# Score products of a Mamba-2 chunk: eight of 128 columns, row tiles innermost, in place of four of 256

## The chip, the cores and the metric

The kernel runs on one core of a Trainium2 chip. The metric is device time in microseconds (us) of one launch, as the median over runs. Engines are named as the profile names them: PE is TensorE's matmul side, PEld its weight loads, DVE is VectorE, ACT is ScalarE, POOL is GpSimd, SP issues most of the DMAs.

## The reference

Two blocks follow each other, all in fp32. The first is a chunked state-space scan over 4 sequences of 768 tokens, 8 heads, head size 32 and state size 16. The second sends its 3072 x 256 result through four experts.

```python
# scan, per chunk of tokens (i, j inside the chunk)
L  = exp(cum[i] - cum[j]) * (i >= j)
CB = einsum('bhin,bhjn->bhij', Cc, Bc)          # the scores
y  = (CB * L) @ xc  +  (Cc @ state) * exp(cum)  # within the chunk + from before it
state = decay_full * state + sum_j decay_from_j * outer(Bc, xc)
# experts, x = y as (3072, 256)
p = domain_probs / sum(domain_probs)
for e in range(4):
    out += p[:, e] * (relu(x @ w1[e]) @ w2[e])  # w1: 256 x 1024, w2: 1024 x 256
```

## The kernel before

The scan is done in 24 chunks of 128 tokens (`c`), four chunks to a block of 512 tokens (`k`, six blocks). The experts are done per block in eight steps (`n`, 48 in all): each step takes one expert and one part of its hidden units. From step 2 on, the two layers are done with seven products each in place of eight (`fmul`, `smul`, with sums of weights made by POOL and sums of activations by DVE); the first two steps are plain. Products of the first layer go to the PSUM banks `X` and `Y`, those of the second are summed in four banks `acc0` to `acc3`. Two more banks (`att`) serve the scan.

The order of the work on every engine is the order of the source (a manual schedule): nothing is moved by a planner. The main loop at line 734 runs over `n`; chunks of the next block enter at steps 0, 2, 4 and 6 (`c_in`) and leave a step later (`c_out`).

A chunk goes through these functions:

- `masks` (L357, ACT) makes `ctm`: C transposed (8 heads x 16 states = 128 rows, 128 tokens), twice. In copy `t` only the rows of heads with parity `t` are kept, so that a group of 32 rows (`q`, two heads) yields one head's scores for each `t`.
- `scores` (L366, PE) makes the scores. A product of group `q` has the 32 x 128 block of B as its stationary operand and the 32 rows of `ctm` as the moving one. It runs in a row tile of the array (`tile_position=(32 * q, 0)`), and the four groups write four different PSUM banks, `g`. From chunk 4 on the banks are `att`, `att`, `X`, `Y`.
- `masked` (L376, DVE) multiplies each `g` by the decays `LT` into `MT`; from chunk 4 on in the order of q = 2, 3, 0, 1, so that `X` and `Y` are read first.
- `outputs` (L389 and L395, PE; L401 and L404, ACT) makes the chunk's outputs. L395 works in column tiles: eight products, `t` outside and `q` inside, of 144 columns (128 in the last block).

In the main loop `scores` and `masked` stand behind `smul(n - 1, 2)` and ahead of `diff(n, "T3", ...)`, `smul(n - 1, 4)`, and the next step's `opened` (`fmul` 1 into `X`, `fmul` 2 into `Y`). Every fp32 product that is no transpose shows in the profile as two weight loads and two matmuls, called two passes here: the 96 score products are 192 records.

The gate of the first expert is spread by four products of 128 columns with stationary operands of 128 columns in the full height of the array (L278, `spread_gate`, 96 rows).

Of the kernel before, what the change touches and what calls it, by code (L numbers as in the profile page):

```python
# [8 lines left out]
FP32 = mybir.dt.float32  # L9
# [3 lines left out]
P = 128  # L13
NQ, NT = 4, 2
# [3 lines left out]
def kernel(  # L18
# [37 lines left out]
    nc = tc.nc  # L56
# [10 lines left out]
    OB, OBT, OCT = DM, DM + HN, DM + 2 * HN  # L67
# [119 lines left out]
    for t, queue in enumerate((nc.sync, nc.scalar)):  # L187
        queue.dma_start(
            out=a_q.rearrange("(q r) c t s -> q r c (t s)", q=NQ)[:, t],
            in_=a.rearrange("(i k) (q t) s -> k q i (t s)", k=NBLK, t=NT)[0][:, 0:SPREAD])  # L190
    nc.scalar.dma_start(
        out=a_sb, in_=a.rearrange("c h s -> (c h) s").rearrange("(p r) s -> p r s", r=2))
# [166 lines left out]
    def scores(c, homes):  # L359

        s = st[c]
        s["g"] = []
        for q, (pool, tag) in enumerate(homes):
            k = slice(32 * q, 32 * q + 32)
            g = pool.tile([P, NT, P], FP32, tag=tag, name="g")
            nc.tensor.matmul(  # L366
                out=g.rearrange("p t s -> p (t s)"), lhsT=s["xb"][k, OBT:OBT + P],
                rhs=s["ctm"][k].rearrange("p t s -> p (t s)"),
                start=True, stop=True, tile_position=(32 * q, 0))
            s["g"].append(g)  # L370

    def masked(c, qs):
        s = st[c]
# [270 lines left out]
    homes = ((ps_s, "acc0"), (ps_s, "acc1"), (ps_att, "att"), (ps_att, "att"))  # L644
# [12 lines left out]
    turn(1, 1)  # L657
    masks(0)
    scores(0, homes)
    decays(0)  # L660
    spread(1)
# [4 lines left out]
    decays(1)  # L666
    turn_gates()
    scores(1, banks)
    masks(2)
    spread(2, (0,))  # L670
# [10 lines left out]

    plain_first(0, 1, (0,))
    scores(2, homes)
    plain_first(0, 1, (1,))
    decays(2)
# [48 lines left out]
    for n in range(PLAIN, NS):  # L734
        k, r = divmod(n, SPB)
# [131 lines left out]
```

## Time and profile before

| | |
|---|---|
| median of 6 runs | 657.29 us (656.55 to 659.99) |
| the profiled execution | 656.26 us, its span 654.5 us |
| granted TensorE clock, mean | 0.998 |
| PE busy | 645.7 us (99% of the span), 3367 records |
| PEld busy | 541.9 us (83%), 3367 records |
| DVE, ACT, POOL busy | 483.9, 115.8, 109.9 us |
| score matmuls (L366) | 192 records, median 478 ns, first at 6.8 us, last at 531.4 us |

The span is the time from the first to the last instruction; the launch's own time is 1.76 us longer. A matmul's record is longer than its turn in the array, since matmuls are pipelined: four matmuls in a row of 256 columns show as 379 ns each, but start 216 ns apart. So starts are read here, not durations. A record of a first matmul behind a change of tiling begins together with its weight load.

### The profile page before, as it was taken

The numbers are of one execution on the slowest core, as the hardware profiler recorded it, in microseconds if no ns is written. First come the engines' busy times: TensorE is split into PE (matmuls) and PEld (weight loads), VectorE is DVE, ScalarE is ACT, GpSimd is POOL, SyncE is SP. The second block draws the span as 40 slices with busy tenths as digits, with TensorE's granted clock in tenths as the row PEclk, the third lists the DMA queues.
The fourth block names the chain that finished last, engine by engine and source line by source line (L and its number), as shares of the span: only waits on it lengthen the run. The fifth ranks groups of instructions, "written<-read, shape, count | busy, mean of one in ns | idle before, by whom it ended". The sixth has DMA issues, their size and how long they took to land.

```text
span 654.5 us, 8922 instructions
## 1 busy us (share of the span) xinstructions
PE 645.7 (99%) x3367; PEld 541.9 (83%) x3367; DVE 483.9 (74%) x814; ACT 115.8 (18%) x247; POOL 109.9 (17%) x157
## 2 busy tenths in 40 slices
PE   8999989999999999999999999999999999999997
PEld 5788868888888888888888888888888888888886
DVE  8679879779686687786867867768777676756555
ACT  2111111221112122111221121112211212111110
POOL 4798383020000002000002000000100000100000
PEclk9999999999999999999999999999999999999999
DMA  7979999542767451666843478536066553156000
GB/s 233 330 274 362 316 383 346 201 162 84 237 197 289 176 192 55 213 235 232 254 162 122 131 247 279 195 130 242 13 239 205 225 187 129 59 162 223 0 1 32
DMA packets 68138, 126.83 MB, mean 194 GB/s; under 512 B 26600, under 2 KB 50048, under 8 KB 68096
## 3 DMA queue, kind: packets, MB, share of 16 engines
q1 hardware_dynamic: 65152, 111.10, 49.6%
q0 software_dynamic: 2304, 14.68, 5.6%
q8 instruction: 26, 0.43, 0.3%
q10 hardware_dynamic: 640, 0.49, 0.2%
q14 instruction: 16, 0.13, 0.1%
HBM read 108.18 MB, written 18.07 MB: 193 GB/s over the span
## 4 chain that ended last, share of the span: by engine, by line
PE 95%; DMA 2%; POOL 1%; DVE 0%; issue 0%; SPq 0%; ACT 0%; POOLq 0%
PE acc L534 41%; PE X L449 23%; PE Y L449 18%; PE g L366 3%; PE y L395 2%; PE acc L515 2%; DMA wt<-in_w_dram 1%; PE y L389 1%; PE X L498 1%; PE Y L498 1%; PE a L309 1%; DMA xb<-in_xbc_dram 1%; POOL wt L161 0%; POOL wt L162 0%; POOL wt L160 0%
## 5 line engine op out<-in xcount | busy, mean ns | idle before, releaser
L461 DVE TENSOR_TENSOR z<-Y,snap 128x512 f32<-128x512 f32 x138 | 94.7, 686 | 127.5 <-ACT snap L456 83.1
L534 PE MATMUL acc<-hT,wt 128*128 128x256 f32 x736 | 183.1, 382 | 0.0
L456 ACT COPY snap<-X 128x512 f32<-128x512 f32 x138 | 80.9, 586 | 466.3 <-PE X L449 466.3
L534 PEld LDWEIGHTS acc<-hT,wt 128*128 128x128 f32 x736 | 138.3, 190 | 24.0 <-issue 6.0
L449 PE MATMUL X<-yS,wt 128*128 128x256 f32 x552 | 141.7, 379 | 0.0
L534 PE MATMUL acc<-h,wt 128*128 128x256 f32 x552 | 141.5, 379 | 0.0
L534 PEld LDWEIGHTS acc<-h,wt 128*128 128x128 f32 x552 | 104.9, 190 | 14.3
L449 PEld LDWEIGHTS X<-yS,wt 128*128 128x128 f32 x552 | 104.9, 190 | 14.3
L471 DVE SCALAR_TENSOR_TENSOR h<-z,gate 128x512 f32<-128x512 f32 x138 | 97.5, 707 | 3.5 <-PE acc L515 0.4
L449 PE MATMUL Y<-yT,wt 128*128 128x256 f32 x368 | 94.5, 379 | 0.0
L449 PEld LDWEIGHTS Y<-yT,wt 128*128 128x128 f32 x368 | 68.6, 189 | 10.8 <-DVE z L461 0.2
L478 DVE TENSOR_TENSOR hT<-h,hT 128x512 f32<-128x512 f32 x92 | 66.5, 722 | 1.6
L478 DVE TENSOR_TENSOR hT<-h,h 128x512 f32<-128x512 f32 x92 | 63.9, 719 | 0.8
L343 DVE TENSOR_TENSOR_SCAN LT<-ab,ident 128x512 f32<-128x512 f32 x42 | 52.4, 1248 | 0.1
L449 PE MATMUL Y<-yS,wt 128*128 128x256 f32 x184 | 49.3, 390 | 0.0
L348 POOL TENSOR_TENSOR MT<-xb,LT 128x128 f32<-128x128 f32 x20 | 8.6, 429 | 240.5 <-PE Y L449 125.4
L449 PE MATMUL X<-yT,wt 128*128 128x256 f32 x184 | 47.2, 379 | 0.0
L376 DVE TENSOR_TENSOR MT<-g,LT 128x256 f32<-128x256 f32 x96 | 34.0, 417 | 16.5 <-PE g L366 16.4
L329 POOL TENSOR_TENSOR cts<-ctm,dec 128x256 f32<-128x256 f32 x20 | 19.7, 983 | 155.5 <-ACT snap L456 155.5
L449 PEld LDWEIGHTS Y<-yS,wt 128*128 128x128 f32 x184 | 33.3, 189 | 8.1 <-issue 4.2
L471 DVE SCALAR_TENSOR_TENSOR h<-X,gate 128x512 f32<-128x512 f32 x50 | 34.3, 686 | 7.7 <-PE X L449 4.1
L449 PEld LDWEIGHTS X<-yT,wt 128*128 128x128 f32 x184 | 35.0, 190 | 4.8
(94 smaller groups left out, 339.4 us busy)
## 6 DMA issues: line engine op xcount, KB each, us to landing
wt<-w_d SPq DMA_DIRECT2D x80, 896.0 KB, 8.9
w_d<-wt POOLq DMA_DIRECT2D x16, 896.0 KB, 6.4
ab<-acut_d SPq DMA_DIRECT2D x21, 512.0 KB, 6.1
wt<-in_w_dram SPq DMA_DIRECT2D x32, 256.0 KB, 6.2
xb<-in_xbc_dram SPq DMA_DIRECT2D x24, 320.0 KB, 5.0
gate<-p_d SPq DMA_DIRECT2D x23, 256.0 KB, 8.3
out_dram<-ot SPq DMA_DIRECT2D x160, 16.0 KB, 4.8
ah<-ac_d SPq DMA_DIRECT2D x20, 64.0 KB
```

Of the source, the lines that this page charges most:

```text
L329: nc.gpsimd.tensor_mul(cts, s["ctm"], dec.unsqueeze(1).to_broadcast([HN, NT, P]))
L343: nc.vector.tensor_tensor_scan(out=LT[:, i * w:i * w + w], data0=s["a"][i], data1=ident.rearrange("p h s -> p (h s)")[:, :w], initial=0.0, ...
L366: nc.tensor.matmul(out=g.rearrange("p t s -> p (t s)"), lhsT=s["xb"][k, OBT:OBT + P], rhs=s["ctm"][k].rearrange("p t s -> p (t s)"), start ...
L376: nc.vector.tensor_mul(s["MT"][:, h, 0:P], s["g"][q], s["LT"][:, h])
L395: nc.tensor.matmul(out=y[32 * q:32 * q + 32, t, 0:w], lhsT=xb[:, h * D:h * D + D], rhs=MT[:, NT * q + t, 0:w], start=(first and t == 0), s ...
L449: nc.tensor.matmul(out=f[bank][:, j], lhsT=wt1[n][:, w, j * P:j * P + P], rhs=rhs, start=(i in (1, 2, 5) and j == 0), stop=(j == JJ - 1), ...
L456: nc.scalar.copy(out=s, in_=first[n]["X"])
L461: nc.vector.tensor_add(z, first[n]["Y"], first[n][i])
L471: nc.vector.scalar_tensor_tensor(out=h, in0=first[n][src], scalar=0.0, in1=g.unsqueeze(1).to_broadcast([P, JJ, HB]), op0=ALU.max, op1=ALU. ...
L478: nc.vector.tensor_sub(h[o], h[x], h[y])
L498: nc.tensor.matmul(out=f[bank][:, j], lhsT=wt1[n][:, w, j * P:j * P + P], rhs=yT[k][:, i, cols], start=(i == 0 and j == 0), stop=(i == 1), ...
L534: nc.tensor.matmul(out=acc[k, u][:, half], lhsT=w2_op(n, w)[:, j], rhs=rhs[:, j], start=(begins and j == 0), stop=(n % SPB == SPB - 1 and ...
```

## The change

The four `g` tiles are allocated first. Then the products are issued with `t` outside and `q` inside, each over one `t` half of the moving operand and of the tile: eight products of 128 columns in place of four of 256. The stationary operand of a group is the same for both `t`, and is loaded for each product. Only the product with `t == 0` has the start flag; both have the stop flag.

```diff
         s = st[c]
         s["g"] = []
-        for q, (pool, tag) in enumerate(homes):
-            k = slice(32 * q, 32 * q + 32)
-            g = pool.tile([P, NT, P], FP32, tag=tag, name="g")
-            nc.tensor.matmul(
-                out=g.rearrange("p t s -> p (t s)"), lhsT=s["xb"][k, OBT:OBT + P],
-                rhs=s["ctm"][k].rearrange("p t s -> p (t s)"),
-                start=True, stop=True, tile_position=(32 * q, 0))
-            s["g"].append(g)
+        for pool, tag in homes:
+            s["g"].append(pool.tile([P, NT, P], FP32, tag=tag, name="g"))
+        for t in range(NT):
+            for q, g in enumerate(s["g"]):
+                k = slice(32 * q, 32 * q + 32)
+                nc.tensor.matmul(
+                    out=g[:, t], lhsT=s["xb"][k, OBT:OBT + P], rhs=s["ctm"][k, t],
+                    start=(t == 0), stop=True, tile_position=(32 * q, 0), skip_group_check=True)
```

## The prediction

> **What bounds the kernel now.** I read the page's busy shares first, then its chain, then the timeline around one chunk's scores.
>
> ```profile
> PE 645.7 (99%) x3367; PEld 541.9 (83%) x3367; DVE 483.9 (74%) x814; ACT 115.8 (18%) x247; POOL 109.9 (17%) x157
> ...
> PE 95%; DMA 2%; POOL 1%; DVE 0%; issue 0%; SPq 0%; ACT 0%; POOLq 0%
> PE acc L534 41%; PE X L449 23%; PE Y L449 18%; PE g L366 3%; PE y L395 2%; PE acc L515 2%; DMA wt<-in_w_dram 1%; PE y L389 1%; PE X L498 1%; PE Y L498 1%; PE a L309 1%; DMA xb<-in_xbc_dram 1%; POOL wt L161 0%; POOL wt L162 0%; POOL wt L160 0%
> ```
>
> TensorE is the bound nearly everywhere: a nanosecond added to the scores (3% of the chain) moves the end by a nanosecond, unless something else waits there. 24 chunks pass, so 0.3% of the median, 1.97 us, is 82 ns per chunk. That 0.3% is also about what a measurement of this kernel can tell from no change.
>
> Next, PE's timeline around the scores of a chunk of the main loop, then the matmuls and loads of L366 that lie in six short stretches (number in brackets: records that overlap the stretch):
>
> ```profile
> 136.82 0.38 PE L534 MATMUL acc<-h,wt 128*128 128x256 f32 x1
> 137.13 0.71 PE L366 MATMUL g<-ctm,xb 32*128 32x256 f32 x8
> 137.77 0.70 PE L534 MATMUL acc<-hT,wt 128*128 128x256 f32 x2
> ```
>
> ```profile
> core 0: us, PE busy (x) PEld busy (x), PEclk, DMA share, GB/s
> 137.12:137.16 0.04, 0.03 (x4) 0.03 (x4) 1.00 0.51 205
> 137.16:137.23 0.07, 0.07 (x4) 0.07 (x4) 1.00 0.56 227
> 137.23:137.26 0.03, 0.03 (x4) 0.03 (x8) 1.00 1.19 495
> 137.26:137.44 0.18, 0.18 (x4) 0.18 (x8) 1.00 0.52 208
> 137.44:137.48 0.04, 0.04 (x8) 0.00 (x0) 1.00 0.00 0
> ```
>
> The eight passes of the four products run as two rounds of four. All four row tiles start within 20 ns (137.12 to 137.16); the loads of the second pass start 107 ns later (137.23 to 137.26); the second four matmuls start at 137.45, which is 0.32 us after the first records: a load of 107 ns and a stream of 256 columns of 213 ns. So the tiles already run side by side, and the second round's loads already hide under the first round's streams. The burst, start to start, takes 644 ns (137.13 to 137.77): 107 load, 2 x 213.5 stream, 20 stagger of the four tiles, 90 until the next tiling's first load. Record by record, 21 of the 24 chunks show these numbers within 1 ns.
>
> **What a round of 128 columns costs.** What remains is whether a round of half the columns takes half the time: its stream is 107 ns, as long as its load. Two places show neighbouring cases: four products of 128 columns with full loads of 128 columns (L278), and eight products in column tiles, `t` outside and `q` inside as in the change (L395).
>
> ```profile
> 15.31 0.97 PEld L278 LDWEIGHTS gp<-p_sb,ident 96*128 96x128 f32 x8 [0.23 <-issue]
> ```
>
> ```profile
> 143.58 0.70 PE L395 MATMUL y<-MT,xb 128*32 128x144 f32 x16
> 144.21 1.13 PE L449 MATMUL Y<-yS,wt 128*128 128x256 f32 x4
> ```
>
> L278: eight loads in 0.97 us, the last one 190 ns long, so seven steps in 0.78 us: 111.4 ns a step. Load and 128-column stream overlap there, and the pair costs 4.5 ns more than the load alone. L395: sixteen passes in four rounds. The last record is 286 ns, so the last start is 0.41 us after the first: a load of 27 ns (32 columns), three steps of 122 ns, a stagger of 20 ns. 144 columns stream in 120 ns at the rate of 256 in 213.5, so the rounds cost 2 to 3 ns beyond their streams. That row shows that eight products in tiles with this loop order fall into rounds of four, and that twice as many instructions keep the 20 ns stagger.
>
> **The sum, part by part.** Removed: two streams of 213.5 ns per chunk, 427 ns. Added: four rounds in their place, with eight more loads and eight more matmuls (192 each over the kernel). A round costs 107 ns if only the stream counts, and 213.5 ns if four row tiles that load while four others stream take as long as the trace can hide: the second round's loads had 213 ns to finish in, and the trace does not show when within it they were done. I take the L278 step, 111.4 ns: it has the same load, the same stream and the same overlap, only the tiling differs; the loads of the first round, four at once, took 107 ns as well, so that tiles loading side by side do not slow each other. The burst then is 107 load + 3 x 111.4 + 107 last stream + 20 stagger + 90 until the next load = 658 ns, against 644: +14.5 ns. The ends are +1 ns (3 x 107) and +320 ns (3 x 213.5 and the last stream 107).
>
> Over the kernel: 23 chunks x 14.5 ns = 0.33 us. Chunk 0 runs at half the clock (its second round starts 588 ns after the first in place of 320), so its share doubles to about 0.03 us or a little more. In chunks 3 and 4 a bank comes free late, and the last tiles start 0.65 us and 0.40 us after the first; the late tiles then need four rounds in place of two, +14.5 ns again, while the early tiles' second halves ride along. In all +0.4 us; by the ends 0.0 and +7.7 us.
>
> The allocation of the four tiles ahead of the products costs nothing: each bank's wait stays with its group's first product. What is new is that a wait of group 2 or 3 now has second halves queued behind it that did not exist before; in the main loop no such wait shows (all four start within 20 ns), and where one shows (chunks 3, 4) it is priced above.
>
> Who waits for the scores: DVE, idle 0.92 us ahead of `masked` in the main loop.
>
> ```profile
> 137.92 1.42 DVE L376 TENSOR_TENSOR MT<-g,LT 128x256 f32<-128x256 f32 x4 [0.92 <-PE g L366]
> 138.53 0.84 PEld L449 LDWEIGHTS X<-yT,wt 128*128 128x128 f32 x4
> 138.74 1.03 PE L449 MATMUL X<-yT,wt 128*128 128x256 f32 x4
> ```
>
> The first mask reads `X` until about 138.34, and PE writes `X` again from 138.74: 0.4 us of room. Since DVE and PE shift together with the burst's end, +14.5 ns is not felt; the next `Y` (139.60, its mask done at 138.67) has more room still. No DMA, ACT or POOL instruction moves.
>
> So the profiled execution would go from 654.5 to 654.9 us of span and from 656.26 to 656.7 of its own time. The median of the runs is 1.03 us above that execution: 657.29 + 0.4 = 657.7.
>
> [...]
>
> **The rivals.**
>
> *Loads only partly hidden (slower).* Four tiles loading while four stream has 107 ns to hide in instead of 213, and no row shows it at that pace. If a load under streams takes longer than alone, each of three steps grows. It decides from a step of 134 ns (111.4 + (82 - 14.5)/3). The price reaches from there to +320 ns per chunk, 7.7 us; the middle, a step of 160 ns, is +3.9 us, 661.2. Against it: L278's full-height step of 111.4, and loads under streams that show 184 ns as records against 181 without. For it: nothing but the missing row.
>
> *The second halves do not join the burst (slower).* If TensorE doesn't let a tile's second product follow while other tiles still work, one more drain and load fall between `t = 0` and `t = 1`: 90 + 107 = 0.2 us per chunk, 4.7 us, 662.0. L395 speaks against it: there the second `t` follows without a gap. It is column tiles, though, with loads of 27 ns.
>
> *Less around the burst (faster).* The last full matmul's stream ends at 137.03 (136.82 + 0.216) and the next begins at 137.88 (137.77 + a load of 0.107): 0.85 us, of which 0.43 are streams, so 0.42 are not. Around L395 the same reading (143.06 + 2 x 0.216 = 143.49 to 144.32) gives 0.83 - 4 x 0.122 = 0.34. If smaller products had the smaller share, 77 ns x 24 = 1.8 us would go, 655.5, at the edge of the bound. Most of that difference is the first load (107 against 27 ns), which stays.
>
> That the change doesn't do what it says (loads left out because the stationary operand repeats) is nearly excluded: between two loads of one operand three others come, and it would give at most the forecast's 0.4 us back.
>
> **How the numbers follow.** Forecast case 0.62, its own range 656.3 to 659.0 (both ends of the small terms and the runs' scatter). Partly hidden loads 0.20, spread from 659.3 to 665.0. Second halves apart 0.10, near 662.0. Faster 0.08. So faster by over 0.3% is 0.08, within 0.3% 0.62, slower 0.30. The range 656.0 to 663.0 leaves out most of the faster case and the dearer part of the partly hidden loads, together 0.15 to 0.2. The prediction is the likeliest case's 657.7.
>
> **What would show it.** In the changed kernel L366 has 384 matmul records and 384 loads. Right: sixteen passes in four rounds, starts 111 ns apart, the burst from first L366 record to the next L534 record 0.66 us, DVE's wait ahead of `masked` within 0.03 us of 0.92. Partly hidden: rounds 134 ns or more apart. Apart: a gap of 0.2 us inside the burst between the eighth and the ninth matmul. Wrong altogether: a burst of 0.66 us and yet a time outside 655.3 to 659.3, or a new wait of PE for `X` or `Y`.

## Result and the profile after

The changed kernel takes 657.96 us (median of 36 runs, 656.3 to 660.19), against 657.23 us of the kernel before (78 runs). The ratio is 1.0015 with a 95% interval of 1.0010 to 1.0021: 0.15% slower, +1.0 us (0.7 to 1.4), inside the 0.3% that the prediction counts as no change. The profiled execution took 657.68 us, its span 655.9 us.

The page of the changed kernel, busy shares and chain:

```profile
PE 645.6 (98%) x3559; PEld 547.2 (83%) x3559; DVE 482.0 (73%) x814; ACT 115.8 (18%) x247; POOL 110.9 (17%) x157
...
PE 94%; DMA 2%; DVE 2%; SPq 1%; issue 1%; POOL 0%; ACT 0%; POOLq 0%
```

192 matmuls and 192 loads more, and TensorE is still the bound. The same burst as in the prediction (chunk 8, in the main loop), on PE's timeline, and its score records in short stretches (in brackets the records that overlap each):

```profile
137.81 0.59 PE L534 MATMUL acc<-h,wt 128*128 128x256 f32 x2
138.33 0.73 PE L368 MATMUL g<-ctm,xb 32*128 32x128 f32 x16
138.99 0.48 PE L534 MATMUL acc<-hT,wt 128*128 128x256 f32 x1
```

```profile
138.32:138.36 0.04, 0.03 (x4) 0.03 (x4) 1.00 0.42 179
138.36:138.43 0.07, 0.07 (x4) 0.07 (x4) 1.00 0.34 125
138.43:138.47 0.04, 0.04 (x4) 0.04 (x8) 1.00 0.08 26
138.54:138.58 0.04, 0.04 (x8) 0.04 (x8) 1.00 0.08 26
138.65:138.69 0.04, 0.04 (x12) 0.04 (x8) 1.00 0.04 13
138.76:138.80 0.04, 0.04 (x12) 0.04 (x4) 1.00 0.08 26
```

Four matmul records overlap at first, eight in the second round and twelve from the third on (a record, median 270 ns, is longer than its turn of 107 to 112 ns a round), and a new four begins every 0.11 us; the rounds' loads lie under the streams of the round before. Record by record, the first load takes 107 ns, the loads of the rounds begin 109 and then 112 ns apart, and the next L534 begins 657 ns after the first score record, against 644 before: +13 ns. DVE waits 0.90 us for the scores, as before (0.92):

```profile
139.11 1.42 DVE L376 TENSOR_TENSOR MT<-g,LT 128x256 f32<-128x256 f32 x4 [0.90 <-PE g L368]
```

**Nothing else grew from chunk 7 on.** The bursts of chunk 7 and chunk 23 (the last) on PE's timeline, first of the kernel before, then of the changed one:

```profile
110.86 0.71 PE L366 MATMUL g<-ctm,xb 32*128 32x256 f32 x8
...
531.04 0.71 PE L366 MATMUL g<-ctm,xb 32*128 32x256 f32 x8
```

```profile
112.05 0.73 PE L368 MATMUL g<-ctm,xb 32*128 32x128 f32 x16
...
532.43 0.73 PE L368 MATMUL g<-ctm,xb 32*128 32x128 f32 x16
```

From the one to the other are 420.18 us before and 420.38 after: 0.20 us for 16 bursts, 13 ns each (12.5 at the rows' rounding). From chunk 7 to the end of the span it is 654.47 - 110.86 = 543.61 against 655.86 - 112.05 = 543.81. The profiles of the runs below agree: 543.60 to 543.62 us wherever chunks 7 to 23 have four products, 543.81 to 543.82 wherever they have eight in this order. What the two profiled executions differ by otherwise, 1.2 of 1.4 us, lies ahead of 112 us.

**Where it lies.** At 88 us PE waits for chunk 6's `cts` (C times the decays, the moving operand of the product at L389), which POOL makes late, behind sums of weights. PE's timeline of the kernel before has there 2.55 us:

```profile
90.41 0.70 PE L389 MATMUL y<-cts,M 128*128 128x256 f32 x2 [2.55 <-POOL cts L329]
```

and the changed kernel's has 2.55 us too:

```profile
89.96 0.70 PE L389 MATMUL y<-cts,M 128*128 128x256 f32 x2 [2.55 <-POOL cts L329]
90.59 0.99 PE L395 MATMUL y<-MT,xb 128*32 128x144 f32 x16
91.51 2.08 PE L449 MATMUL Y<-yS,wt 128*128 128x256 f32 x4
```

POOL is late because a transfer of weights (`wt<-in_w_dram`) lands near 80 us. The first sum of weights that waits for it, on POOL's timeline, before and then after:

```profile
80.26 0.72 POOL L160 TENSOR_TENSOR wt<-wt 128x256 f32<-128x256 f32 x1 [9.49 <-DMA wt<-in_w_dram]
```

```profile
79.74 0.72 POOL L160 TENSOR_TENSOR wt<-wt 128x256 f32<-128x256 f32 x1 [9.13 <-DMA wt<-in_w_dram]
```

From there POOL needs 10.1 and 10.2 us to the end of `cts`. In the kernel before, the chain that ends this wait goes back over POOL's sums, that transfer (70.99 to 80.09 us), its issue and DVE to PE's own work up to 68 us.

The four L449 matmuls behind the wait take 2.08 us in the changed kernel; with nothing in their way four take 1.13. The clock was halved: busy times and granted clock of two stretches of the changed kernel (PE, PEld, DVE, ACT, POOL; then the clock):

```profile
87.45:90.85 3.40, 0.89 (x10) 0.56 (x14) 3.37 (x3) 0.00 (x0) 3.00 (x6) 1.00 1.01 422
90.86:94.26 3.40, 3.40 (x23) 2.42 (x14) 0.98 (x3) 0.46 (x2) 3.00 (x5) 0.50 1.02 426
```

The halved stretch lasts 3.41 us and pushes all later products back by 1.6 us (from the wait's end to chunk 7 it is 22.09 us, against 20.45).

The start differs too, and also by the clock. Eight matmuls of L309, behind chunk 0's scores, on PE's timeline before and after:

```profile
7.95 3.30 PE L309 MATMUL a<-a_q,qmask 128*128 128x256 f32 x8
```

```profile
6.89 1.99 PE L309 MATMUL a<-a_q,qmask 128*128 128x256 f32 x8
```

The trace's record of the full clock begins at 10.64 us before and at 5.52 us after, which is ahead of the first changed instruction (6.12 us). Chunk 1 begins at 11.29 and 10.54 us.

So the profiled pair differs by bursts (+0.2 from chunk 7 on), by the halved stretch (+1.6), and by a start that is 0.45 us ahead when the wait ends. Only the first belongs to the change for certain. The runs that follow ask how much of the measured +1.0 us it is.

### The profile page after: what moved, and what is told of

Read it like the earlier page. It is cut to its first block, busy times and chain, and to the rows that moved or that the text cites. A ratio compares the mean times of both kernels' runs of the same rounds, so it can differ in the third digit from the quotient of the medians.

```text
span 655.9 us, 9306 instructions
## 1 busy us (share of the span) xinstructions
PE 645.6 (98%) x3559; PEld 547.2 (83%) x3559; DVE 482.0 (73%) x814; ACT 115.8 (18%) x247; POOL 110.9 (17%) x157
## 4 chain that ended last, share of the span: by engine, by line
PE 94%; DMA 2%; DVE 2%; SPq 1%; issue 1%; POOL 0%; ACT 0%; POOLq 0%
PE acc L534 41%; PE X L449 23%; PE Y L449 18%; PE y L395 2%; PE g L368 2%; PE acc L515 2%; DMA wt<-in_w_dram 2%; PE y L389 1%; PE X L498 1%; PE Y L498 1%; DMA wt<-w_d 1%; DVE LT L343 1%; DVE h L471 0%; PE t L651 0%; SPq L133 0%
## 5 line engine op out<-in xcount | busy, mean ns | idle before, releaser
L534 PE MATMUL acc<-hT,wt 128*128 128x256 f32 x736 | 183.1, 382 | 0.0
L534 PEld LDWEIGHTS acc<-hT,wt 128*128 128x128 f32 x736 | 138.3, 190 | 20.2
L449 PE MATMUL X<-yS,wt 128*128 128x256 f32 x552 | 142.1, 380 | 0.0
L534 PE MATMUL acc<-h,wt 128*128 128x256 f32 x552 | 141.5, 379 | 0.0
L449 PEld LDWEIGHTS X<-yS,wt 128*128 128x128 f32 x552 | 105.3, 191 | 14.5
L534 PEld LDWEIGHTS acc<-h,wt 128*128 128x128 f32 x552 | 104.9, 190 | 14.3
L449 PE MATMUL Y<-yT,wt 128*128 128x256 f32 x368 | 94.5, 379 | 0.0
L449 PEld LDWEIGHTS Y<-yT,wt 128*128 128x128 f32 x368 | 68.7, 190 | 10.7 <-DVE z L461 0.2
L478 DVE TENSOR_TENSOR hT<-h,hT 128x512 f32<-128x512 f32 x92 | 65.0, 706 | 1.6
L449 PE MATMUL Y<-yS,wt 128*128 128x256 f32 x184 | 50.2, 396 | 0.0
L449 PE MATMUL X<-yT,wt 128*128 128x256 f32 x184 | 47.2, 379 | 0.0
L449 PEld LDWEIGHTS Y<-yS,wt 128*128 128x128 f32 x184 | 33.8, 192 | 8.5 <-issue 3.9
L449 PEld LDWEIGHTS X<-yT,wt 128*128 128x128 f32 x184 | 35.0, 190 | 4.8
```

The source lines that it names most:

```text
L449: nc.tensor.matmul(out=f[bank][:, j], lhsT=wt1[n][:, w, j * P:j * P + P], rhs=rhs, start=(i in (1, 2, 5) and j == 0), stop=(j == JJ - 1), ...
L478: nc.vector.tensor_sub(h[o], h[x], h[y])
L534: nc.tensor.matmul(out=acc[k, u][:, half], lhsT=w2_op(n, w)[:, j], rhs=rhs[:, j], start=(begins and j == 0), stop=(n % SPB == SPB - 1 and ...
```

## Experiments

Each run carries the mean granted clock. In the profiled executions a mean of 0.996 or 0.997 goes with the halved stretch behind the wait and one at the end of the kernel; 0.998 to 1.0 goes with at most the one at the end (the changed kernel's 0.996: half clock from 90.85 to 94.27 us and from 654.05 us; the 0.998 of the kernel before: from 652.34 us alone). The other runs are sorted by this; the few at 0.993 or 0.994 were not profiled. Ratios are to the kernel before, run on the same chip.

**Theory A**: the bursts are all that the change costs; the rest is the halved stretch, which falls more often. **Theory B**: something in the start of the kernel became slower.

### The kernel before, once more (no edit)

> The kernel of before, unchanged, as a control with the granted clock of every run. Both theories: ratio 1.000 within 0.0005. Theory A (the burst costs 13 ns in each of 24 chunks, what the first six cost is swallowed by PE's 2.5 us wait for POOL's cts in chunk 5, so the change itself is worth 18 x 13 ns = 0.24 us; the rest of the measured +1.0 us comes from a 3.4 us stretch at half clock behind that wait, which falls more often in the changed kernel): runs here with a mean clock of 0.998 to 1.0 are more than the 5 in 36 of the changed kernel, and are 1.3 to 1.7 us shorter than those at 0.996. Theory B (the rest is a new delay in the start of the kernel, chunks 0 to 5): the clocks are spread as in the changed kernel.

Measured: ratio 1.0001 (0.9991 to 1.0010). Over all sets of runs the kernel before has 110 runs with their clocks, 29 of them (26%) at 0.998 or more; the changed kernel 6 of 48 (12%). In this set the kernel before had a median of 656.3 us at 0.998 or more and one of 657.2 at 0.996 to 0.997. So the halved stretch was more frequent in the runs of the changed kernel, but it is the rule in both: 14% more runs x 1.6 us are 0.2 us, not 0.7. And over all sets the changed kernel is still 0.6 us behind at 0.996 to 0.997 (657.98 against 657.37), and 0.8 us at 0.998 or more (656.98, of six runs, against 656.21). Theory A doesn't explain all.

### Eight products in chunks 0 to 5 only, and from chunk 6 on only

```diff
+        if c <= 5:          # e3: if c > 5
+            for t in range(NT):
+                for q, g in enumerate(s["g"]):
                     ...
```

> Eight products only in chunks 0 to 5, four products from chunk 6 on. Theory A: no direct cost (0.0 us, swallowed by the wait for POOL), only a share of the half-clock stretch, so +0.0 to +0.7 us with all of it in runs at a lower clock. Theory B: +0.7 us at equal clock.

> Eight products only from chunk 6 on (18 chunks), four before. Both theories: 18 x 13 ns = +0.24 us at equal clock, and the burst from the first score record to the next L534 record 657 ns in place of 644. Theory A: the frequency of the half-clock stretch is that of before. A later delay that the profile did not show would give more than +0.3 us.

Measured: early 1.0011 (1.0001 to 1.0022), +0.7 us; late 1.0005 (0.9994 to 1.0017), +0.3 us. The late part agrees with what its 18 bursts are worth, 0.24 us, within an interval of -0.4 to +1.1 us. The early part has six bursts, 0.08 us, and more than they explain, though the interval reaches down to them. That speaks for theory B. But the early kernel's profile doesn't show where: its wait at 88 us ended at 89.72 us, earlier than in either profile of the kernel before (90.41, and 90.9 in the control); that of the late kernel, which has four products in the start, ended at 90.01.

### The changed kernel, once more (no edit)

> The changed kernel again, beside the others on the same chip: +0.7 to +1.4 us as measured, the sum of the early and the late part. Theory A: at equal clock only +0.24 us.

Measured: 1.0014 (1.0005 to 1.0023), the first result again. Its profile has the wait (until 90.17 us) and the halved stretch as well. At equal clock (0.996 to 0.997) it is +0.8 us over the kernel before beside it (658.01 against 657.21), not +0.24: against theory A.

### PE's wait taken away, at the wrong chunk

```diff
-            nc.gpsimd.tensor_mul(
+            (nc.vector if c == CPB + 1 else nc.gpsimd).tensor_mul(
                 s["MT"][:, :, P:], ...
-                nc.gpsimd.tensor_mul(cts, ...
+                (nc.vector if c == CPB + 1 else nc.gpsimd).tensor_mul(cts, ...
```

> The kernel of before (four products), with the two POOL multiplications of chunk 5 (L329, L348) on DVE, so that PE doesn't wait 2.5 us for them. Both theories: PE's wait at L389 of chunk 5 goes, and with it the half-clock stretch behind it: 1.5 to 3.5 us less than before (about 654 to 655.5), and no run with a clock under 0.997, unless another wait for POOL's weight sums takes its place.

> The changed kernel (eight products) with the same two multiplications on DVE. Theory A: without the wait and the half-clock stretch nothing is left but the bursts, 24 x 13 ns = 0.32 us over the same edit of before. Theory B (the rest of the measured +1.0 us lies in the order of the start or elsewhere): +0.7 us or more over it.

Measured: four products 658.69 us, 1.0012 (0.9996 to 1.0028), eight 658.40 us, 1.0016 (1.0002 to 1.0029); 9 of 12 and 9 of 11 runs have a clock under 0.998. Both expectations missed: I had counted the chunks wrongly, and the wait at 88 us is for chunk 6. The profile of the eight products still has it, 2.33 us long, with the halved stretch. That of the four, one of the three runs at a higher clock (654.88 us), has only 0.22 us of it, since POOL's sums began at 77.94 us there. These runs say nothing on the two theories.

### The same, at chunk 6

The edit is that above with `c == CPB + 2`.

> The kernel of before with the two POOL multiplications of chunk 6 (L329 and L348) on DVE. It is chunk 6 whose outputs wait at 88 us for POOL's cts; the last two runs had moved those of chunk 5, which nothing waits for. Theory A: the wait of 2.3 to 2.9 us goes, and the half-clock stretch of 3.4 us behind it, worth 1.6 us, goes in nearly all runs: 653 to 655 us, no run with a clock below 0.997, and a smaller scatter. If POOL's late sums of weights are what holds PE, the wait moves to a later place and less than 1 us is gained.

> The changed kernel with the same edit for chunk 6. Theory A: with the wait and the half-clock stretch gone, the difference to the same edit of before is the bursts alone, 24 x 13 ns = 0.32 us (0.0 to 0.6 with the scatter). Theory B (0.4 us or more beside the bursts, in the start of the kernel): 0.7 us or more.

> The same kernel as in the last call (four products, chunk 6's two multiplications on DVE) once more, to have twice the runs: 655.0 to 655.6 us, clocks of 0.997 to 1.0.

> Eight products with the same edit once more. Theory A: over both calls the eight products are 0.1 to 0.6 us behind the four (24 bursts of 13 ns are 0.32). Theory B: 0.7 us or more.

Measured: four products 655.26 and 654.27 us, ratios 0.9961 (0.9948 to 0.9975) and 0.9961 (0.9947 to 0.9976); eight products 655.57 and 655.21 us, ratios 0.9970 (0.9959 to 0.9981) and 0.9978 (0.9966 to 0.9990). All but one of the 36 runs have a clock of 0.998 or more. PE's timeline where the wait was, four products:

```profile
87.41 1.03 PE L535 MATMUL acc<-h,wt 128*128 128x256 f32 x4
88.27 0.59 PE L390 MATMUL y<-cts,M 128*128 128x256 f32 x2
88.79 0.70 PE L396 MATMUL y<-MT,xb 128*32 128x144 f32 x16
```

The four products' first time is just above the 653 to 655 us expected, their second below the 655.0 to 655.6. The wait and the halved stretch are gone in all four profiles; 0.7 to 1.6 us of new waits of PE for DVE (`z`, at 92 to 94 and 105 to 106 us) take part of the gain. By the means, eight products are 0.50 us behind four in the first pair (655.53 against 655.04) and 0.91 in the second (655.23 against 654.32), 0.7 together (0.3 to 1.1 by resampling the runs of each). 0.32 us, the 24 bursts, lies at the lower end of this, and theory B's 0.7 in its middle. In the four profiles the stretch from chunk 7's burst to the end is 543.60 and 543.61 us for four products and 543.82 for eight, both times: the main loop is settled to 0.01 us, the start is not.

The kernel before with this edit beats both kernels that were compared: by the ratio 0.39% less time, 2.6 us, both times. The edit has nothing to do with the scores.

### The order of the loops

```diff
-        for t in range(NT):
-            for q, g in enumerate(s["g"]):
+        for q, g in enumerate(s["g"]):
+            for t in range(NT):
```

> Eight products again, but with the group outside and t inside, so that a row tile's two products follow one another. If a row tile queues all four passes of its group, the rounds of four stay and a burst is 657 ns plus up to 20 ns of stagger: +0.3 to +0.8 us of direct cost. If the loads of a tile's third and fourth pass block the instructions behind them, the groups start one after another, some 330 ns apart, and a burst takes about 1.6 us: +24 us.

Measured: 1.0027 (1.0013 to 1.0041), +1.8 us (0.9 to 2.7). A burst of chunk 8 on PE's timeline:

```profile
139.18 0.75 PE L368 MATMUL g<-ctm,xb 32*128 32x128 f32 x16
139.86 0.70 PE L534 MATMUL acc<-hT,wt 128*128 128x256 f32 x2
```

677 ns, record by record, 20 more than with the row tiles innermost: the tiles' first matmuls start 13.4 ns apart in place of 6.7, and the rounds stay. A tile's four passes don't hold up the other tiles. The stated part of the change, row tiles first, is worth 20 ns per chunk, 0.5 us; from chunk 7 to the end the profile has 544.17 us, 0.35 more than with the row tiles innermost, 21 ns for each of 17 bursts. The result as a whole was above the expected +0.3 to +0.8 us; the rest would lie ahead of chunk 7, where the profile's wait at 88 us was 3.3 us long.

### Sixteen products of 64 columns

```diff
-        for t in range(NT):
+        for t in range(2 * NT):
             for q, g in enumerate(s["g"]):
-                    out=g[:, t], ... rhs=s["ctm"][k, t],
+                    out=g.rearrange("p t s -> p (t s)")[:, h], ...   # h: 64 columns
```

> Sixteen products of 64 columns, row tiles innermost: eight rounds of loads of 107 ns over streams of 53 ns. If the load sets the step of a round (111.4 ns as in the changed kernel), a burst is 107 + 7 x 111.4 + 53 + 20 + 90 = 1050 ns, +406 over 644: +9.7 us. If the stream sets it, about 670 ns: +0.6 us.

Measured: 1.0131 (1.0103 to 1.0159), +8.6 us (6.8 to 10.4). A burst:

```profile
144.57 1.12 PE L368 MATMUL g<-ctm,xb 32*128 32x64 f32 x32
145.62 0.48 PE L535 MATMUL acc<-hT,wt 128*128 128x256 f32 x1
```

1050 ns, to the nanosecond what a step of 111.4 ns gives. With half the columns the step of a round stays at 111.6 ns: it isn't the stream that sets it, and the load, 107 ns, is what stayed. A limit on the number of instructions is unlikely: a step of L278 has one load and one matmul, a round here four of each, and both take 111 to 112 ns. So at 128 columns load and stream are level (107 ns each), and the change costs 13 ns a burst; at 64 columns each added round costs its whole step of 111.6 ns. From chunk 7 to the end the profile has 550.51 us, 6.9 more than before, 406 ns for each of 17 bursts. The +9.7 us of all 24 bursts lie inside the measured interval; the profile still has a wait of 1.94 us for POOL's `cts`, so how much of the first seven bursts arrives isn't known.

## Why the prediction was right, and where it fell short

**The burst: right.** The sum gave 658 ns and +14.5 ns; the trace has 657 and +13, in 21 of 24 chunks. The step taken from L278 (111.4 ns) is nearly the step of the row tiles: the matmuls of the four rounds start 107, 111 and 112 ns apart once the first load is taken off, 330 ns in place of the 334 summed. The tail from the last stream to the next load is 93 ns in place of 90.

**Loads only partly hidden: fell.** Four tiles that load while four stream keep the pace of one: 107 to 112 ns a round, against 111.4 ns a step at L278. With sixteen products they keep it over eight rounds in a row, at 111.6 ns. **Second halves apart: fell.** The ninth matmul, the first of the third round, starts 111 ns after the first of the second, a round's step without a gap, and the rounds stay even with the loop order turned round (677 ns a burst). **Less around the burst: fell.** From the end of the burst's last stream to the next load it is 93 ns, against 90 before, and the first load still takes 107 ns.

**The total: inside the range, but too small, and in part by luck.** +0.4 us was summed, +1.0 (0.7 to 1.4) measured. The median of 657.96 us lies in the forecast case's own 656.3 to 659.0, yet only about 0.2 of the 1.0 us is shown to be what the sum describes: the 17 bursts from chunk 7 on, the same in every profile. Two steps of the prediction were off.

The first is the term put at nothing, "No DMA, ACT or POOL instruction moves". PE waits about 2.5 us for POOL at 88 us, the one long wait of PE in the chain's middle, which the prediction doesn't mention. It ended between 89.7 and 90.9 us in the profiles of four and eight products whose chunks 5 and 6 are left as they were, behind a transfer that lands near 80 us, and a halved stretch worth 1.6 us followed it in some of them and not in others. Such shifts from run to run are larger than the sum.

The second is "a nanosecond added to the scores moves the end by a nanosecond". It fails the other way: chunk 6's burst isn't in the chain that ends the wait, which is POOL's own from that transfer on, so its 13 ns go into the wait while there is one. The six first bursts, 0.08 us, stand ahead of the transfer and may; no run here can tell.

What is known of the 1.0 us: the 17 bursts, 0.2 us; the halved stretch in 14% more of the runs, 0.2 us by the clocks. That eight products draw this stretch more often by more than chance wasn't shown: in all four profiles of the kernels with eight products of 128 columns that have it the record of the full clock begins at 5.5 to 6.1 us, before the first changed instruction, and in the traces of both kernels the clock's later changes lie whole multiples of 3.4133 us behind that point (see the last section). The other 0.6 us (0.3 to 1.0) lies ahead of chunk 7 and its cause stays open. The run with only the early chunks changed points to the start, and without the wait the eight products are 0.7 us behind (0.3 to 1.1). But the profiles don't show it: leaving out the edit of chunk 5, those with eight products in the start reach chunk 6's burst at 81.1 to 81.4 us, those with four at 81.4 to 82.2, and the one of these at 81.4 is the only one whose full clock began early (5.8 us), as it did in all of those with eight. No profile of four products with the halved stretch was kept, so the pair at equal clock is missing.

**Chunk names.** The late bank at 54 us belongs to chunk 5, not 4 as the prediction has it. That burst was priced at +14.5 ns; it took 1278 ns in the changed kernel's profile and 991 in its repeat, 1034 in the kernel before and 1262 in its control: it ends when DVE frees a bank, and the products follow, so that no 14.5 ns can be read from it. Chunk 0, which the prediction has at half the clock, ran at full clock in the changed kernel's profile (765 ns, against 1.17 us in the kernel before).

## What to carry to other kernels

In this kernel, whose loads of weights lie under streams, the cost of splitting a product came from comparing the two. At 128 columns, where the stream is as long as the load (107 ns each), the split cost 13 ns a burst; at 64 columns the step stayed at 111.6 ns, so each added round cost more than a whole load. Narrower products were not measured. A neighbouring row of the same trace (L278, a small helper product in the start, 111.4 ns a step) had the step to 1%. And before a nanosecond on the bound engine is counted in full, look for that engine's own waits behind it: one of 2.5 us was here worth more than the change, and taking it away gained 2.6 us.

## What the runs showed of the hardware

**Behind a wait of 2.5 us the clock was halved in some executions and not in others.** Two executions had waits of 2.55 us: in one the clock was 0.50 for 3.41 us afterwards, in the other it stayed at 1.00. It stayed at 1.00 behind the control's wait of 2.84 us, and was halved behind one of 2.33 us (the eight products with chunk 5's edit), so the wait's length alone doesn't tell. In the traces of both kernels the clock's changes are 3.4133 us or a whole multiple of it apart: 641.71 us in the kernel before, which is 188 of them, and 85.33, 3.413 and 559.79 us in the changed one, which are 25, 1 and 164. So the profile can be cut into such stretches, counted from the moment at which the full clock's record begins. In the changed kernel PE was busy for 0.89 of 3.40 us in the stretch ahead of the halving (1.18 in its repeat, 1.08 behind the wait of 2.33 us); in the last stretch ahead of the half clock at the end it was 1.34 us in the kernel before and 1.04 in the changed one. In the kernel before, counted from 10.64 us, the wait straddles two stretches:

```profile
85.73:89.13 3.40, 2.13 (x10) 1.52 (x9) 3.37 (x4) 0.59 (x1) 3.00 (x5) 1.00 0.81 291
89.14:92.54 3.40, 2.13 (x22) 1.50 (x23) 3.12 (x4) 0.46 (x2) 3.24 (x5) 1.00 1.02 424
```

2.13 busy in each, and the clock stays at 1.00; in the control's it was 2.19 and 1.77. So in these executions half clock followed stretches with 0.89 to 1.34 us of busy PE, 26 to 39% of the time, and didn't follow those with 1.77 or more. Why the clock does so isn't shown.

**The row tiles started side by side in each of the three orders that ran.** A group's passes stand together in the source order in the kernel before and in the run with the group outside, and yet the four groups' first passes start side by side (within 20 ns, and within 3 x 13.4 = 40), ahead of the first group's second pass (0.32 us after the first in the kernel before). The order shows only in the distance of these starts: 6.7 ns where a group has four instructions in a row (two loads, two matmuls), 13.4 ns where it has eight.
